# Pool's additions, their stores and a table load placed behind the next group's combinations

## The chip, the cores and the metric

The kernel runs on one core of one Trainium2 chip. The metric is device time in microseconds (us): the median of several executions. TensorE (PE in the profile, its weight loads PEld) multiplies matrices; VectorE (DVE), ScalarE (ACT) and GpSimd (POOL, called Pool here) work beside it, and SyncE (SP) issues most DMAs.

## The reference

The computation has two parts. First linear attention over batch 8, 8 heads, 576 tokens and head size 64; then an FNet block over the heads laid side by side (width 512):

```python
q_s = softmax(q, axis=-1); k_s = softmax(k, axis=2)        # each with + 1e-9 in the denominator
kv = einsum('bhsd,bhse->bhde', k_s, v)
x = einsum('bhsd,bhde->bhse', q_s, kv)                     # -> (B, S, H*D) = (8, 576, 512)

mixed = real(fft(fft(x, axis=1), axis=2))
u = x + mixed
un = (u - mean(u)) / sqrt(var(u) + 1e-6)                   # over the 512 columns
ch = relu(un @ w_ch1) @ w_ch2                              # 512 -> 2048 -> 512
return u + ch
```

## The kernel before, in words

The tokens are worked in nine groups of 512. Groups 0 to 7 hold 512 of the 576 tokens of one batch element each; group 8 (`B`) holds the 64 left over of all eight. They run in the order 0 to 6, 8, 7. While group g runs its two large products on TensorE, the attention, the Fourier mixing and the normalisation of later groups are worked in between.

Matrix products use a Strassen-Winograd scheme with seven products instead of eight; `ORDER = (1, 6, 5, 7, 2, 4, 3)` is the order of the seven. For the first product of a group (`up`, L1366, un @ w_ch1 and relu) the transposed, normalised u of the group lies in the tile `unT` in seven blocks: blocks 0 to 3 are quarters of u, and blocks 4, 5, 6 and a new block 1 are differences of them, 4 = 1 - 0, 1 = 3 - 1, 5 = 3 - 4, 6 = 2 - 5. `B_AT` says which block a product reads: m=1 block 0, m=6 block 5, m=5 block 4, m=7 block 1, m=2 block 2, m=4 block 6, m=3 block 3. `up` makes four passes (j = 0 to 3) over these seven products. Three PSUM banks carry them: ba (m=1, then m=2), bb (m=6, then m=7, then m=4, on top of each other) and bc (m=5, then m=3). Between two products of one bank DVE reads the bank (u2 and u3 at L1336, other results at L1377), so the next product of that bank waits for this reading.

The second product (`deep_down`, the matmuls of L1463 and L1493) is a Strassen scheme of two levels for the groups after group 1. The outer products come as 1, then the pairs (2, 4), (7, 6), (5, 3). The results of an inner scheme are put together by DVE (L1500) and ACT (L1507, L1514) into blocks of the tile `big`. From there they are added into `x`, which holds u, by `into` (L1443, 128x512 elements each); `sums` (L1446) adds two such blocks. Both run on `E`, which is Pool, except for the last two groups, where it is DVE. The list `after` gives each such step a time after its pair. Then `store` sends the finished rows out: rows in order go straight to `out_dram`, reversed ones through a DRAM tile `mirror`. Group 8's rows are put on a list, `later`, which `timed` empties during the last group, 36 DMAs, one every 1.2 units.

`norm(g)` prepares `unT` for a group while the group before is still in `deep_down`. DVE transposes 32x32 blocks (L1213) into spare blocks of `unT`; 32 small copies (`moved`, L1221), shared between ACT and Pool, put them in place; then `combine` (L1227) and `combine_last` (L1232) make the differences. `back` (L1181) has ACT load the table of the exponential again after the square root. At the same time the key part of a later attention runs (`keys`): maxima on DVE (L696), two exchanges of the maxima between partitions (ACT L676 and L679, each followed by a minimum on DVE, L683), exponentials on ACT (L700), transposes on DVE (L709), and matmuls (L716). The q part begins with a maximum (L757 on DVE) and a subtraction on Pool (L762).

The order of all this is written out by hand. Every step is a pair of a time in units and a function; a group takes 106 units. All steps are sorted by time and issued in that order, so each engine runs its own instructions in the order of these times, and waits, by semaphores, for what others have not finished. Times are not enforced; only the order counts. At a group's end the order of the steps of Pool, DVE and ACT, in units from the end of `deep_down` (which is the start of the next group's `up`), is:

```text
Pool  sums 7+6 at -9, into(1,0,7) at -7 among the copies of u (-11 to -5.3), into(1,1,7) at -5,
      block 1 at -3.9, into(1,1,5) at +1, into(0,1,5) at +2, into(0,1,3) at +4
DVE   blocks 4 and 5 at -3.9, L683 at -2.8, L1500 (bank bb) at -2.5, L683 at -1.6, L1500 (bc) at -0.5
ACT   table load at -11.9, copies of u until -5.3;   SP  stores at +3.5, +4.5, +7, +8
```

Of the kernel before, what the change touches and what calls it, by code (L numbers as in the profile page):

```python
# [43 lines left out]
ALU = mybir.AluOpType  # L44
# [75 lines left out]
def at(t, script):  # L120
    return [(t + dt, step) for dt, step in script]


def tokens(c, u):

    a = {(0, 0): 1, (0, 1): S - P, (1, 0): S // 2 - P, (1, 1): S // 2 + 1}[c, u]
    return slice(a, a + P)
# [11 lines left out]
class _Block:  # L139
# [1017 lines left out]
    def norm(self, g):  # L1157

        nc, V = self.nc, self.nc.vector
# [63 lines left out]
        def combine():  # L1223
            if g > 0:
                some = lambda i: self.unT[g][:, i]
                for e, to, x, y in ((V, 4, 1, 0), (nc.gpsimd, 1, 3, 1), (V, 5, 3, 4)):
                    e.tensor_tensor(out=some(to), in0=some(x), in1=some(y), op=ALU.subtract)  # L1227

        def combine_last():
            if g > 0:  # L1230
                some = lambda i: self.unT[g][:, i]
                V.tensor_tensor(out=some(6), in0=some(2), in1=some(5), op=ALU.subtract)  # L1232

        steps = []
        put = lambda t, f, *a: steps.append((t, lambda: f(*a)))
        if g > 1:
            for c in range(2):
                t = 7.5 * c
                for n, i in enumerate((c, c + 2)):
                    put(t + n, stats, i)  # L1240
                    put(t + 4.2 + n, normal, i)
                    put(t + 5.5 + n, turned, i)
                put(t + 2, root, slice(c, 4, 2))
                put(t + 3.2, scales, slice(c, 4, 2))
                for n in range(16):
                    put(t + 7.2 + .4 * n, moved, c, n % 4, n // 4)
            put(7.5 + 6.6, back)
            put(7.5 + 8.2 + 16 * .4, combine)
            put(7.5 + 18.2 + 16 * .4, combine_last)
            return steps  # L1250
        if g == 0:
# [13 lines left out]
        for n, i in enumerate((0, 2, 1, 3)):  # L1265
            put(9.3 + 1.3 * n, normal, i)
            put(11.8 + 1.3 * n, turn, i)
            put(12.6 + 1.3 * n, laid, i)
        put(17.5, combine)
        put(27.5, combine_last)  # L1270
        return steps
# [141 lines left out]
    def deep_down(self, g, order):  # L1413

        nc, V, G = self.nc, self.nc.vector, self.nc.gpsimd
        base, last, skip = self.base[order] + NP, order == B, self.first_deep(order)
# [8 lines left out]
        box, steps = {}, []  # L1425
# [22 lines left out]
        def store(t, u):  # L1448
            for c in range(2):
                steps.extend(at(t + c, self.store(g, c, u, lambda c=c: self.xpart(g, c, u))))  # L1450
# [25 lines left out]
        def half(t, c, u, d, wait=9):  # L1476
            x = lambda: self.xs[g, u][:, c, d * HD:(d + 1) * HD]
            steps.extend(at(t, self.store(g, c, u, x, d, wait)))
# [23 lines left out]
        def ends(unit, n):  # L1502
# [14 lines left out]
            if n == 3:  # L1517
                plus(out(1), "bc", "u2")

        after = {(2, 4): [(7, into, 1, 0, 4), (9, into, 0, 0, 2)],  # L1520
                 (7, 6): [(1, sums, 6, 1), (3, into, 0, 1, 6), (5, sums, 7, 6), (7, into, 1, 0, 7), (9, into, 1, 1, 7)],
                 (5, 3): [(0.6, into, 1, 1, 5), (1.2, into, 0, 1, 5), (1.8, into, 0, 1, 3)] if last else
                         [(1, into, 1, 1, 5), (2, into, 0, 1, 5), (4, into, 0, 1, 3)]}
        names = {1: ("bb", "bb"), 2: ("bc", "bb"), 4: ("ba", "bb")}
        n, t = 2 * len(ORDER), 0
        for i, unit in enumerate(order):
# [28 lines left out]
        if last:  # L1555
            half(t - 8 + 2, 1, 1, 1)
            half(t - 8 + 3, 0, 0, 1)
            half(t - 8 + 3.1, 1, 0, 1, 3)
        else:
            store(t + 3.5, 1)  # L1560
            store(t + 7, 0)
        return steps

    def down(self, g, order):
# [66 lines left out]
    def store(self, g, c, u, x, d=None, wait=9):  # L1631


        nc, own = self.nc, g < B
        e = nc.sync if d is None or c else nc.scalar
        s = slice(0, D) if d is None else slice(d * HD, (d + 1) * HD)
        if not own:
            def later():
                self.later += [lambda r=r, m=m: e.dma_start(m, x()[r]) for r, m in self.shared(self.out, 2 * (2 * u + c))]
            return [(0, later)]  # L1640
        out = self.out[g, tokens(c, u), s]
        if c == u:
            return [(0, lambda: self.apart(e.dma_start(out, x())))]
        box = []
        cols = lambda a: a.rearrange("t (k n) -> k t n", n=DH)

        def there():
            t = self.dram.tile([P, D], F32, tag="mirror", name="mirror", bufs=4)
            box.append(t[:, s])
            e.dma_start(box[0], x())  # L1650

        return [(0, there), (wait, lambda: self.apart(e.dma_start(cols(out)[:, ::-1, :], cols(box[0]))))]
# [3 lines left out]
def kernel(ctx: ExitStack, tc: tile.TileContext, q, kT, v, w1, w2, ft,  # L1656
                                                           cd, out):
    blk = _Block(ctx, tc, q, kT, v, w1, w2, ft, cd, out)

    def timed(t, order, g):  # L1660
        b = order + 1
        steps = at(t, blk.up(order, g)) + at(t + UP, blk.down(g, order))
        if order == B:
            return steps + [(t + 6 + 1.2 * i, lambda i=i: blk.later and blk.later.pop(0)()) for i in range(36)]
        if b == B:
            return steps + at(t + UP + 16, blk.norm(groups[b]))
        start, end = -7 if order > 2 else 0, 45
        if b + 1 < B:
            steps += at(t, blk.ahead(b + 1))
        steps += at(t, blk.attention_timed(b, start, end)) + at(t + end, blk.folded(b))  # L1670
        t, soon = t + UP, 2 * (order == 1)
        for i, k in enumerate((2, 3, 0, 1, 4)):
            steps += at(t + soon + (1.7 if order > 1 else 2) * i, blk.block(b, k))
        mixes = [blk.mix_own(b, c) for c in range(2)]
        if b % 2:
            mixes.insert(0 if b == B - 1 else 2, blk.mix_shared(b // 2))
        for i, some in enumerate(mixes):
            steps += at(t + 9.2 + 1.65 * soon + 3.2 * i, some)
        return steps + at(t + 24 + 1.65 * soon, blk.norm(groups[b]))
# [31 lines left out]
    steps = blk.opening(fetch, converted)  # L1711
# [3 lines left out]
    t = first + second  # L1715
# [28 lines left out]
    t = 0  # L1744
    for order, g in enumerate(groups[1:], 1):
        later += timed(t, order, g)
        t += UP + (TWICE if order > 1 else UP)
# [59 lines left out]
```

## Time and profile before

| | us |
|---|---|
| median of 3 runs (lowest, highest) | 1047.89 (1046.48, 1051.24) |
| the profiled execution's own time | 1048.45 |
| its span on the core | 1046.7 |
| PE busy | 1027.1 |
| DVE busy | 744.1 |
| ACT busy | 495.3 |
| POOL busy | 445.7 |
| granted TensorE clock, share of full | 0.998 |

The span is the time from the first to the last instruction of the program in the profiled execution. Busy times are of one engine each, and they overlap. In the list of waits a line names who waited, for whom, the total, how often, and the longest. In the timeline a line has the start, the length, the engine, the line of the kernel, what is written and read, the shapes, the count of instructions merged into the line, and in brackets the idle time before it with what ended it. In the table of windows the columns are the window, its length, then the busy time (and instructions) of PE, PEld, DVE, ACT and POOL, the granted clock, the DMA engines' mean busy share and the GB/s moved.

### The profile page before, as it was taken

What the parts mean: (1) busy time and instruction counts of PE and PEld (TensorE: products, weight loads), DVE (VectorE), ACT (ScalarE), POOL (GpSimd) and SP (SyncE); (2) the same over time, 40 slices, a digit from 0 to 9 for tenths busy, and PEclk for the clock granted to TensorE, in tenths of its full rate; (3) what the DMA queues carried; (4) which work ended last, traced back from release to release, by engine and by line L of the source; (5) the groups of instructions that cost most, each with busy time, mean ns of one, the idle gap of its engine ahead of it and who ended that gap; (6) DMA issues with size and microseconds to landing.
All of it is one profiled execution on the core that took longest, in us unless ns stands there. A gap on an engine that the chain in (4) does not pass through costs nothing.

```text
span 1046.7 us, 16845 instructions
## 1 busy us (share of the span) xinstructions
PE 1027.1 (98%) x6066; PEld 888.5 (85%) x6066; DVE 744.1 (71%) x1452; ACT 495.3 (47%) x1246; POOL 445.7 (43%) x448
## 2 busy tenths in 40 slices
PE   8999999999999999999999999999999999999998
PEld 7844554888888898889988998989898998999898
DVE  5898888775766897677776787579757754694463
ACT  5674532862449227842675256823682242151210
POOL 3164420366543736554736555474656470040000
PEclk9999999999999999999999999999999999999999
DMA  8787598587999566955786577747644674575464
GB/s 259 254 264 259 173 257 291 181 243 232 330 303 231 201 247 228 244 197 192 258 217 196 200 253 244 198 178 262 218 167 161 224 259 161 213 278 204 171 228 144
DMA packets 114315, 236.02 MB, mean 225 GB/s; under 512 B 23272, under 2 KB 78696, under 8 KB 103608
## 3 DMA queue, kind: packets, MB, share of 16 engines
q1 hardware_dynamic: 113864, 234.42, 68.4%
q8 instruction: 48, 0.79, 0.3%
q14 instruction: 35, 0.29, 0.1%
q10 hardware_dynamic: 288, 0.26, 0.1%
q0 software_dynamic: 80, 0.26, 0.1%
HBM read 199.79 MB, written 39.06 MB: 228 GB/s over the span
## 4 chain that ended last, share of the span: by engine, by line
PE 72%; DVE 9%; DMA 3%; ACT 3%; POOL 2%; issue 1%; SPq 0%; DVEq 0%; ACTq 0%; POOLq 0%
PE bb L1366 15%; PE ba L1366 9%; PE bc L1366 9%; PE bb L1493 8%; PE ba L1493 5%; PE bb L1463 5%; PE bc L1493 5%; PE bb L1582 2%; PE acc L791 2%; PE acc L716 2%; PE acc L1088 2%; PE acc L1091 1%; PE bc L1582 1%; PE ba L1582 1%; DMA big<-w1s 1%
## 5 line engine op out<-in xcount | busy, mean ns | idle before, releaser
L1366 PE MATMUL bb<-unT,big 128*128 128x256 f32 x768 | 182.7, 380 | 5.8 <-DVE big L1500 3.3
L1366 PEld LDWEIGHTS bb<-unT,big 128*128 128x128 f32 x768 | 143.8, 190 | 27.3 <-DVE big L1500 4.9
L1378 ACT ACTIVATE big<-big 128x512 f32<-128x512 f32 x96 | 60.3, 629 | 157.0 <-DVE big L1377 156.0
L775 ACT ACTIVATE qT<-q 32x128 f32<-32x128 f32 x384 | 117.9, 307 | 13.8 <-DVE q L765 8.7
L1366 PE MATMUL ba<-unT,big 128*128 128x256 f32 x512 | 124.0, 379 | 0.0
L1366 PE MATMUL bc<-unT,big 128*128 128x256 f32 x512 | 121.9, 380 | 0.0
L1366 PEld LDWEIGHTS bc<-unT,big 128*128 128x128 f32 x512 | 96.0, 190 | 13.5 <-DVE big L1377 1.1
L1366 PEld LDWEIGHTS ba<-unT,big 128*128 128x128 f32 x512 | 94.5, 190 | 12.0 <-issue 0.5
L1493 PE MATMUL bb<-big 128*128 128x128 f32 x848 | 104.2, 276 | 0.4 <-DVE u L1500 0.3
L1336 DVE TENSOR_TENSOR u<-bb,s 128x512 f32<-128x512 f32 x66 | 45.4, 689 | 81.6 <-PE bb L1366 68.6
L1493 PEld LDWEIGHTS bb<-big 128*128 128x128 f32 x848 | 98.9, 192 | 1.5 <-DVE u L1500 1.0
L1443 POOL TENSOR_TENSOR x<-x,big 128x512 f32<-128x512 f32 x45 | 59.9, 1340 | 55.9 <-ACT big L1470 18.8
L1221 POOL COPY unT<-unT 32x256 f32<-32x256 f32 x98 | 43.1, 440 | 91.1 <-DVE unT L1213 86.8
L1493 PE MATMUL ba<-big 128*128 128x128 f32 x640 | 78.0, 275 | 0.0
L1493 PEld LDWEIGHTS ba<-big 128*128 128x128 f32 x640 | 75.2, 192 | 0.7
L1439 DVE TENSOR_TENSOR big<-big 128x512 f32<-128x512 f32 x98 | 73.4, 780 | 0.0
L762 POOL TENSOR_TENSOR q<-q,qm 128x512 f32<-128x512 f32 x24 | 25.8, 1074 | 102.3 <-DVE qm L757 50.0
L1221 ACT COPY unT<-unT 32x256 f32<-32x256 f32 x126 | 50.6, 402 | 28.2 <-DVE unT L1213 26.5
L385 POOL TENSOR_TENSOR big<-big 128x512 f32<-128x512 f32 x24 | 30.5, 1270 | 69.4 <-ACT big L1378 69.4
L1463 PE MATMUL bb<-big 128*128 128x256 f32 x256 | 59.5, 380 | 0.0
L1377 DVE TENSOR_TENSOR big<-bc,u 128x512 f32<-128x512 f32 x64 | 44.0, 688 | 19.4 <-PE bc L1366 18.6
L1463 PEld LDWEIGHTS bb<-big 128*128 128x128 f32 x256 | 48.2, 190 | 8.3 <-DVE big L1377 1.1
(282 smaller groups left out, 2040.3 us busy)
## 6 DMA issues: line engine op xcount, KB each, us to landing
big<-w2d SPq DMA_DIRECT2D x67, 1024.0 KB
big<-w1s SPq DMA_DIRECT2D x64, 896.0 KB
big<-w2s SPq DMA_DIRECT2D x16, 1024.0 KB
big<-in_w_dram SPq DMA_DIRECT2D x21, 512.0 KB
w2d<-big SPq DMA_DIRECT2D x42, 256.0 KB
kb<-in_kT_dram SPq DMA_DIRECT2D x24, 320.0 KB
q<-in_q_dram SPq DMA_DIRECT2D x28, 256.0 KB
vt<-in_v_dram SPq DMA_DIRECT2D x36, 160.0 KB
```

The lines of the kernel that those rows point to most:

```text
L385: e1.tensor_tensor(out=to(4), in0=at(2), in1=at(3), op=ALU.add)
L775: nc.scalar.activation(to[t, i * Q:i * Q + Q], one, ACT.Exp)
L1221: copy(to, of)
L1336: plus = lambda t: V.tensor_tensor(out=temp(t), in0=box["bb"][:], in1=box["s1"][:], op=ALU.add)
L1366: nc.tensor.matmul(bank()[:, i, :], lhsT=w[:, WA_AT[m], k * P:(k + 1) * P], rhs=self.unT[g][:, B_AT[m], k, :], start=first and i == 0 and ...
L1377: steps = [(0, lambda: V.tensor_tensor(out=hp(i), in0=bank()[:], in1=u()[:], op=ALU.add)), (0.8, lambda: nc.scalar.activation(hp(i), hp(i) ...
L1378: (0.8, lambda: nc.scalar.activation(hp(i), hp(i), ACT.Relu))]
L1439: e.tensor_tensor(out=to(o), in0=to(x), in1=to(y), op=op)
L1443: E.tensor_tensor(out=x, in0=x, in1=tile(m), op=ALU.add)
L1463: nc.tensor.matmul(box[name][:, i, :], lhsT=h[p][:, A_AT[m], i * P:(i + 1) * P], rhs=self.stream[n][:, p, :], start=p == 0 and (m != 1 or ...
L1493: nc.tensor.matmul(box[place[n]][:, i, :], lhsT=own(m)(A_AT[n])[:, f, :], rhs=w[:, r // 2, r % 2 * P:r % 2 * P + P], start=first and f == ...
L1582: nc.tensor.matmul(bank()[:, i, :], lhsT=h[p][:, A_AT[m], i * P:(i + 1) * P], rhs=w[:, p, :], start=first and i == 0 and p == 0, stop=p == ...
```

## The change

For groups with g > 1 Pool makes block 5 (3 - 4), which was DVE's, and DVE makes block 1 (3 - 1), which was Pool's. Block 1 gets a step of its own, `combine_one`, at +0.6 units. ACT's table load moves behind the copies of u (from -11.9 to -4.7). In all groups but the last the two additions of result 7 leave the place among the copies, and all five additions of the group's end stand at +4, +5.5, +7, +8.5 and +10. The stores move from +3.5 and +7 to +9.5 and +13 (with their second halves one unit later). The list of group 8's stores is emptied from 11 units on instead of 6.

```diff
         def combine():
             if g > 0:
                 some = lambda i: self.unT[g][:, i]
-                for e, to, x, y in ((V, 4, 1, 0), (nc.gpsimd, 1, 3, 1), (V, 5, 3, 4)):
+                for e, to, x, y in ((V, 4, 1, 0), (nc.gpsimd, 5, 3, 4)) if g > 1 else ((V, 4, 1, 0), (nc.gpsimd, 1, 3, 1), (V, 5, 3, 4)):
                     e.tensor_tensor(out=some(to), in0=some(x), in1=some(y), op=ALU.subtract)
+
+        def combine_one():
+            some = lambda i: self.unT[g][:, i]
+            V.tensor_tensor(out=some(1), in0=some(3), in1=some(1), op=ALU.subtract)
...
-            put(7.5 + 6.6, back)
+            put(7.5 + 7.4 + 16 * .4, back)
             put(7.5 + 8.2 + 16 * .4, combine)
+            put(7.5 + 12.7 + 16 * .4, combine_one)
             put(7.5 + 18.2 + 16 * .4, combine_last)
...
-                 (7, 6): [(1, sums, 6, 1), (3, into, 0, 1, 6), (5, sums, 7, 6), (7, into, 1, 0, 7), (9, into, 1, 1, 7)],
+                 (7, 6): [(1, sums, 6, 1), (3, into, 0, 1, 6), (5, sums, 7, 6), *(((7, into, 1, 0, 7), (9, into, 1, 1, 7)) if last else ())],
                  (5, 3): [(0.6, into, 1, 1, 5), (1.2, into, 0, 1, 5), (1.8, into, 0, 1, 3)] if last else
-                         [(1, into, 1, 1, 5), (2, into, 0, 1, 5), (4, into, 0, 1, 3)]}
+                         [(4, into, 1, 0, 7), (5.5, into, 1, 1, 7), (7, into, 1, 1, 5), (8.5, into, 0, 1, 5), (10, into, 0, 1, 3)]}
...
-            store(t + 3.5, 1)
-            store(t + 7, 0)
+            store(t + 9.5, 1)
+            store(t + 13, 0)
...
-            return steps + [(t + 6 + 1.2 * i, lambda i=i: blk.later and blk.later.pop(0)()) for i in range(36)]
+            return steps + [(t + 11 + 1.2 * i, lambda i=i: blk.later and blk.later.pop(0)()) for i in range(36)]
```

## The prediction

> **What bounds the kernel now.** I read the page's engine shares first, then TensorE's waits, then windows over the group ends, then the timeline of one group end engine by engine.
>
> ```profile
> PE 1027.1 (98%) x6066; PEld 888.5 (85%) x6066; DVE 744.1 (71%) x1452; ACT 495.3 (47%) x1246; POOL 445.7 (43%) x448
> ...
> PE bb L1366 <- DVE big L1500: 3.3, 4, 0.9
> PE bb L1366 <- DVE u L1336: 2.5, 4, 0.6
> ```
>
> TensorE is busy for 98% of the span, so only its idle time can be won, and of that 5.8 us are two waits that occur four times each. Both belong to the first products of a new group. The windows give their full price. Each runs from a group's first matmul to the start of its fifth product (m=2):
>
> ```profile
> 404.73:415.90 11.17, 9.65 (x55) 8.31 (x53) 8.46 (x16) 8.30 (x29) 6.15 (x5) 1.00 0.69 256
> 517.05:528.07 11.02, 9.64 (x55) 8.30 (x53) 8.31 (x16) 6.49 (x21) 7.41 (x6) 1.00 0.63 241
> 629.54:640.70 11.16, 9.64 (x54) 8.30 (x53) 8.45 (x16) 8.30 (x29) 6.12 (x5) 1.00 0.72 256
> 741.83:752.86 11.03, 9.65 (x54) 8.31 (x53) 8.32 (x16) 6.50 (x21) 7.43 (x6) 1.00 0.62 238
> 854.64:861.55 6.91, 6.91 (x34) 6.03 (x33) 3.52 (x5) 0.59 (x1) 6.41 (x5) 1.00 0.80 302
> ```
>
> The last row has the same four products without attention work and without a wait: 6.91 us, 1.73 a product. The other four rows also hold two runs of ten attention matmuls (L716), 1.12 us each by the timeline below (526.95 to 528.07). Without waits they would take 6.91 + 2 x 1.12 = 9.15. So they lose 2.02, 1.87, 2.01 and 1.88, together 7.8 us, at a granted clock of 1.00. This is more than the 5.8 of the wait list, because the pipe also restarts after each wait.
>
> The timeline of the second of these ends (first matmul at 517.05), in the order PE, DVE, POOL, ACT:
>
> ```profile
> 517.05 1.89 PE L1366 MATMUL ba<-unT,big 128*128 128x256 f32 x8
> 519.69 1.99 PE L1366 MATMUL bb<-unT,big 128*128 128x256 f32 x8 [0.75 <-DVE big L1500]
> 525.15 1.96 PE L1366 MATMUL bb<-unT,big 128*128 128x256 f32 x8 [0.63 <-DVE u L1336]
> 526.95 1.28 PE L716 MATMUL acc<-vt,kb 128*128 128x129 f32 x10
> ...
> 512.69 2.26 DVE L696 TENSOR_REDUCE km<-kb 128x4 f32<-128x640 f32 x3
> 515.78 2.37 DVE L1227 TENSOR_TENSOR unT<-unT 128x512 f32<-128x512 f32 x2 [0.83 <-POOL unT L1221]
> 518.07 1.23 DVE L683 TENSOR_TENSOR km<-km,across 128x16 f32<-128x16 f32 x1
> 519.22 0.41 DVE L1500 TENSOR_TENSOR big<-bb,s 128x256 f32<-128x256 f32 x1
> 523.59 0.84 DVE L709 STREAM_TRANSPOSE kb<-kb 128x640 f32<-128x640 f32 x1 [0.91 <-ACT kb L700]
> 524.36 0.65 DVE L1336 TENSOR_TENSOR u<-bb,s 128x512 f32<-128x512 f32 x1
> ...
> 513.58 1.27 POOL L1443 TENSOR_TENSOR x<-x,big 128x512 f32<-128x512 f32 x1
> 515.83 1.77 POOL L1443 TENSOR_TENSOR x<-x,big 128x512 f32<-128x512 f32 x1
> 517.56 1.71 POOL L1227 TENSOR_TENSOR unT<-unT 128x512 f32<-128x512 f32 x1
> ...
> 519.33 0.84 ACT L679 COPY across<-km 32x16 f32<-32x16 f32 x4 [3.93 <-DVE km L683]
> 520.41 1.70 ACT L700 ACTIVATE kb<-kb,km 128x160 f32<-128x160 f32 x5 [0.24 <-DVE km L683]
> ```
>
> Stall one: product m=6 needs PSUM bank bb, which DVE's L1500 empties only at 519.63. That addition's input was ready near 515.5 (L1493 moves on to bank bc at 515.26), but it stands in DVE's queue behind the two combinations (2.37 us, of which the second takes 1.64 where 0.69 is normal) and a 16-column minimum (L683, 1.23 where its median is 0.18). Both slow ones lie beside Pool's L1443 and L1227 and end just after them: a DVE operation with two SBUF inputs and a Pool operation do not overlap here, one waits for the other. Stall two: m=7 overwrites bb and needs u2 (L1336), which stands behind the key transposes (L709), which need ACT's exponentials (L700), which start at 520.41 because that same minimum was late.
>
> **The change, part by part,** on this group end (times as above).
>
> Pool before the combination. One addition into x (513.58, 1.27) leaves from among the copies of u. The last two copies (0.83) then follow at 513.58 and end at 514.41, not 515.74.
>
> ACT. The table load (1.28) and its dummy activation (0.20) leave from before nine copies, which end at 514.29, and go behind them. The copies end near 512.8, the load fills 512.8 to 514.3, and the next copy (L1514, 514.31) starts as now. Cost nothing; its cover is that L1514 waits for PE's ba anyway.
>
> First combination on DVE (block 4). It is no longer gated by Pool but by DVE's own key maxima, which end at 514.95: 514.95 to 515.65, 0.8 earlier. Block 5, which stood next on DVE, goes to Pool. So L683 follows at 515.7 (its inputs are there: ACT's L676 copies, issued at 514.98, take 0.42) and L1500 at 515.9 to 516.3. Bank bb is free 2.5 us before m=6 wants it at 517.05 + 1.73 = 518.78. Stall one goes.
>
> Block 5 on Pool. It waits for block 4 (515.65). A Pool subtraction of this shape has no undisturbed row; the bounds are 1.27 (L1443 alone) and 1.77 (L1443 beside a DVE combination). Nothing but the short L683 stands beside it, so I take 1.27 to 1.45: done by 517.2, at most 517.5. m=6 reads it at 518.78: hidden, with 1.3 us or more to spare. Behind it in Pool's queue are only the additions into x.
>
> The second stall's chain. ACT's L679 copies run 516.0 to 516.85; the second minimum waits until Pool lets go, about 517.2; L700 starts near 517.5 instead of 520.41. Five exponentials (1.70 with 0.33 a step), the s1 copy (0.56) and three more end near 520.7; the transpose (0.84) ends at 521.5, u2 (0.65) at 522.2. m=7 wants bank bb at 517.05 + 3 x 1.73 + 1.12 = 523.35. Stall two goes with 1.1 us to spare. What is late next is u3, by the same shift at 526.2 to 527, against m=4 at 517.05 + 5 x 1.73 + 2 x 1.12 = 527.9.
>
> Block 1 on DVE (new third combination) stands between L1500's second addition and the first transpose. It takes 0.69, or up to 1.64 if it meets an addition of Pool's: done by 519.1. The first transpose needs four exponentials (518.8), so at most 0.3 us is added there, and m=7 reads block 1 at 523.35. Hidden.
>
> Pool's five additions (1.27 each, 1.77 beside DVE) come at 517.2 and later instead of 513.58 to 524.74. Two run at once, three come behind the next q subtraction (L762, which waits for a DVE maximum), and the last ends near 529. The regions of big they read are next written by the new group's m=3 result (start of its addition 12 us after 517.05) or by Pool itself later in order. Nobody waits.
>
> Stores. SP puts four stores out of x, and two out of mirror, later, behind the four vt loads, which wait for PE (528.26 now, 526.4 then). Four stores at 0.35 to 0.45 us of issue each are out before the weight load that waits for the end of the first pass. The buffers of x are next written by DVE's L804 at 27.8 us after the first matmul; the last mirror copy now leaves at about 14.5 and needs a few us. The stores (4 x 256 KB, about 3 us of transfer) move from a stretch in which the DMA engines are little used (share 0.34 in 526 to 529) toward the full one (1.18 in 543 to 550, 0.97 in 550 to 556). Then they idle (0.29 in 556 to 562.5), before the weights asked for at 548.69 are needed at about 562.5. Room of some 4 us against 3, with weights ahead of vt in the queue: taken as nothing, and kept for a rival.
>
> Other ends. At 293.45, 854.64 and 948.48 TensorE has no wait at the first products; there the move is worth 0, with about 1 us of cover for Pool's block (at 293.45 the present Pool combination ends at 294.36, m=6 starts at 295.18). At 941.23 a wait of 0.26 may go. At 948.48 the five additions are DVE's, and fall into idle gaps of about 2 us. The 36 stores of group 8 start five units later and still end before the last group's w2d loads.
>
> Sum: 7.8 us, against the profiled execution: span 1046.7 to 1038.9, with 1.75 around it 1048.45 to 1040.65. That execution is 0.56 above the median of the three runs, so 1047.89 - 7.8 = 1040.1.
>
> One rule bears against the change. The Trainium skill's page "SBUF — State Buffer", section "SBUF: two separate sides", says that the pair of ports shared by VectorE and GpSimd is an exclusive lock: whichever starts first holds it for the whole instruction, and the other is blocked entirely. The stretched rows above (0.69 to 1.64, 0.18 to 1.23) agree. By it Pool's work packed behind 515.7 would block L683 twice; what that gives is the first rival.
>
> **Rivals.** *Second stall stays.* If Pool's block 5 starts before DVE's first L683, that waits to 517.0, the L679 copies end at 517.9 and the second L683 waits for an addition to 518.4. L700 starts at 518.6, and u2 ends at 523.4 with m=7 wanting 523.35; one more blocked operation (1.27) brings stall two back whole. The gain is then stall one: (519.69 - 518.78) plus about 0.1 of restart, near 1.02 and 1.15 in turn, 4.3 in all: 1043.6. For it: the two L683 slowed to 1.23 in every end. Against: where both wait for the end of the same combination (172.04), DVE's next starts at 172.08 and Pool's at 172.18.
>
> *A wait on Pool replaces stall one.* m=6 waits for block 5 as long as it waits now for the bank; with stall two partly there, 1047 to 1048. It needs Pool 1.3 us later than worked out; nothing in Pool's queue supplies that.
>
> *Slower: weights late.* The moved stores reach the full DMA stretch and push the weights of the fourth pass past 562.5. It decides once they come more than about 4 us later than now; at 3 us moved plus 1.9 of earlier demand it is not out of reach. Each us beyond costs one in each of four groups; 4 us beyond, with the gain of 7.8 given back, is 1047.9 + 16 - 7.8 = 1056. Against: SP's issues of weights wait for PE, not for DMA, and the weights stand ahead of the vt loads, which nobody needs then.
>
> **How the numbers follow.** Both stalls gone 0.72 (own range 1038.5 to 1042.3: from 0.7 more by small waits, to 0.3 to 0.5 left of stall two in each end); only the first 0.14, at 1043.6; replaced 0.06, near 1047.5; slower 0.08, near 1056. About 0.5% (5.2 us, the spread of the runs before) can be told from no change, so faster 0.75 (the first and a little of the second), same 0.17, slower 0.08. The range 1038.2 to 1045 takes in the first two cases and leaves out 0.14.
>
> **What the profile after would show.** Right: no wait of PE on L1500 or on L1336's u at the four ends; windows of about 9.15 us to the fifth product; DVE's L1227 at about 0.69 each, the first 2.1 us before the group's first matmul; L700 about 0.5 after it (3.4 now). Wrong: a PE wait on Pool's L1227, a PE wait on DMA big<-w1s in the fourth pass, or DVE waiting on DMA before L804.

## The result, and the profile after

The changed kernel takes 1038.57 us (median of 6 runs, 1037.82 to 1040.01) against 1047.1 of the kernel before on the same chip (6 runs, 1046.42 to 1051.24): a ratio of 0.9916, 95% interval 0.9898 to 0.9933, or 8.5 us less. 7.8 less had been forecast, from 1047.89. The profiled execution took 1039.82, with a span of 1038.0.

The page's first line on the engines and two lines of the list of TensorE's waits, of the changed kernel:

```profile
PE 1023.7 (99%) x6066; PEld 888.8 (86%) x6066; DVE 736.4 (71%) x1452; ACT 496.1 (48%) x1246; POOL 441.7 (43%) x448
...
PE ba L1371 <- DMA big<-w1s: 1.3, 1, 1.3
...
PE bb L1498 <- DVE u L1505: 0.2, 1, 0.2
```

(The change adds lines: L1371 here is L1366 before, L1505 is L1500, L1341 is L1336, L1448 is L1443, L1498 is L1493, L1383 is L1378; L1231 is the new combination of block 1.) Both waits on bank bb, four times each, are gone. There is one wait that the profile before does not have, for weights. The windows from a group's first matmul to its fifth product (first its length, then the engines' busy time, the granted clock, the DMA share and GB/s):

```profile
405.40:414.53 9.13, 9.13 (x54) 8.30 (x53) 7.60 (x14) 7.73 (x25) 5.27 (x4) 1.00 0.53 202
515.27:524.42 9.15, 9.15 (x55) 8.32 (x54) 7.62 (x14) 5.72 (x17) 5.53 (x5) 1.00 0.47 175
625.89:635.02 9.13, 9.13 (x54) 8.30 (x53) 7.60 (x14) 7.73 (x25) 5.26 (x4) 1.00 0.54 206
735.74:744.90 9.16, 9.16 (x55) 8.33 (x54) 7.63 (x14) 5.73 (x17) 5.54 (x5) 1.00 0.46 170
```

PE is busy for the whole of each window, and each is 9.13 to 9.16 long where 9.15 was forecast. The DMA share in them fell to 0.46 to 0.54 (0.62 to 0.72 before): the four stores out of `x`, which left SP 5.1 to 8.1 us after the first matmul of the second end before, now leave at 10.7 to 14.0, behind the window. The timeline of the second of these ends, whose first matmul is at 515.27 now (517.05 before), PE, DVE, POOL and ACT in turn:

```profile
517.00 1.89 PE L1371 MATMUL bb<-unT,big 128*128 128x256 f32 x8
521.57 1.89 PE L1371 MATMUL bb<-unT,big 128*128 128x256 f32 x8
...
513.09 0.68 DVE L1227 TENSOR_TENSOR unT<-unT 128x512 f32<-128x512 f32 x1
513.69 0.17 DVE L683 TENSOR_TENSOR km<-km,across 128x16 f32<-128x16 f32 x1
513.78 0.42 DVE L1505 TENSOR_TENSOR big<-bb,s 128x256 f32<-128x256 f32 x1
519.60 0.65 DVE L1341 TENSOR_TENSOR u<-bb,s 128x512 f32<-128x512 f32 x1
...
513.85 1.26 POOL L1227 TENSOR_TENSOR unT<-unT 128x512 f32<-128x512 f32 x1 [1.28 <-DVE km L683]
515.08 2.95 POOL L1448 TENSOR_TENSOR x<-x,big 128x512 f32<-128x512 f32 x2
...
515.18 1.70 ACT L700 ACTIVATE kb<-kb,km 128x160 f32<-128x160 f32 x5 [0.45 <-DVE km L683]
```

DVE's first combination, the minimum and the emptying of bank bb now follow each other, and bb is free 2.8 us before m=6 (517.00). Pool starts block 5 only after the minimum, 0.16 later than the minimum starts, and ends it 1.9 us before m=6. ACT's exponentials start 0.09 us before the group's first matmul; they started 3.36 after it. u2 ends at 520.25, 1.3 us before m=7.

For the whole run I put the 6066 matmuls of both profiles side by side, as they come in the same order, and took how far each starts from its counterpart. From the first matmul of group 3 to the last of all the changed kernel gains 9.15 us: 2.44, 1.88, 2.44 and 1.91 in groups 3 to 6, 0.49 in group 8 and nothing in group 7. Ahead of group 3 it is 0.67 behind: 0.35 gained in the opening, where nothing was changed, and 1.02 lost in group 2, by the wait for weights.

### The profile page after: what moved, and what is told of

The parts are those of the page before. It is cut to its first block, busy times and chain, and to the rows that moved or that the text cites. A ratio compares the mean times of both kernels' runs of the same rounds, so it can differ in the third digit from the quotient of the medians.

```text
span 1038.0 us, 16852 instructions
## 1 busy us (share of the span) xinstructions
PE 1023.7 (99%) x6066; PEld 888.8 (86%) x6066; DVE 736.4 (71%) x1452; ACT 496.1 (48%) x1246; POOL 441.7 (43%) x448
## 4 chain that ended last, share of the span: by engine, by line
PE 89%; DVE 5%; DMA 3%; ACT 1%; issue 0%; SPq 0%; POOL 0%; POOLq 0%; DVEq 0%; ACTq 0%
PE bb L1371 15%; PE ba L1371 10%; PE bc L1371 10%; PE bb L1498 10%; PE ba L1498 7%; PE bc L1498 7%; PE bb L1468 5%; PE acc L716 2%; PE bb L1587 2%; PE bc L1308 2%; PE acc L1088 2%; PE acc L791 2%; PE bb L1287 2%; DMA big<-w1s 2%; PE ba L1287 2%; PE bc L1287 2%
## 5 line engine op out<-in xcount | busy, mean ns | idle before, releaser
L1371 PE MATMUL bb<-unT,big 128*128 128x256 f32 x768 | 181.9, 379 | 0.0
L1371 PEld LDWEIGHTS bb<-unT,big 128*128 128x128 f32 x768 | 144.3, 190 | 19.3 <-DVE u L1341 0.5
L1383 ACT ACTIVATE big<-big 128x512 f32<-128x512 f32 x96 | 60.3, 629 | 157.4 <-DVE big L1382 156.4
L1371 PE MATMUL ba<-unT,big 128*128 128x256 f32 x512 | 124.1, 379 | 1.3 <-DMA big<-w1s 1.3
L1371 PE MATMUL bc<-unT,big 128*128 128x256 f32 x512 | 121.7, 379 | 0.0
L1371 PEld LDWEIGHTS bc<-unT,big 128*128 128x128 f32 x512 | 96.1, 190 | 13.2 <-DVE big L1382 0.5
L1371 PEld LDWEIGHTS ba<-unT,big 128*128 128x128 f32 x512 | 94.5, 190 | 13.5 <-DMA big<-w1s 1.5
L1341 DVE TENSOR_TENSOR u<-bb,s 128x512 f32<-128x512 f32 x66 | 45.4, 688 | 84.0 <-PE bb L1371 71.0
L1498 PE MATMUL bb<-big 128*128 128x128 f32 x848 | 104.1, 276 | 0.2 <-DVE u L1505 0.2
L1498 PEld LDWEIGHTS bb<-big 128*128 128x128 f32 x848 | 98.9, 192 | 1.1 <-DVE u L1505 0.6
L1448 POOL TENSOR_TENSOR x<-x,big 128x512 f32<-128x512 f32 x45 | 59.3, 1333 | 49.2 <-ACT big L1475 19.4
L1498 PE MATMUL ba<-big 128*128 128x128 f32 x640 | 78.0, 275 | 0.0
L1498 PEld LDWEIGHTS ba<-big 128*128 128x128 f32 x640 | 75.2, 192 | 0.7
```

Of the source, the lines that this page charges most:

```text
L1341: plus = lambda t: V.tensor_tensor(out=temp(t), in0=box["bb"][:], in1=box["s1"][:], op=ALU.add)
L1371: nc.tensor.matmul(bank()[:, i, :], lhsT=w[:, WA_AT[m], k * P:(k + 1) * P], rhs=self.unT[g][:, B_AT[m], k, :], start=first and i == 0 and ...
L1383: (0.8, lambda: nc.scalar.activation(hp(i), hp(i), ACT.Relu))]
L1448: E.tensor_tensor(out=x, in0=x, in1=tile(m), op=ALU.add)
L1498: nc.tensor.matmul(box[place[n]][:, i, :], lhsT=own(m)(A_AT[n])[:, f, :], rhs=w[:, r // 2, r % 2 * P:r % 2 * P + P], start=first and f == ...
```

## Experiments

Four theories were set against each other. **Port**: DVE's two-input operations and Pool's hold each other up, and the stalls come from what that does to the order of DVE's queue. **Gate**: the gain is the earlier start of the first combination. **Relief**: DVE had one combination too many ahead of the bank. **Chance** is about the wait for weights alone: it comes and goes with the way the transfers fall. Besides each median I give the gain from group 3's first matmul on, by the matmuls side by side, which leaves the opening and group 2 out.

### The table load alone

```diff
-            put(7.5 + 6.6, back)
+            put(7.5 + 7.4 + 16 * .4, back)
```

> The kernel before with ACT's table load alone moved behind the copies of u. Port theory (the stalls come from DVE operations held by Pool's two-input operations): no change, 1047 to 1048, since the first combination is gated by Pool's last copy (515.74 in the profile before), not by ACT's (514.29); ACT's copies end 1.5 us earlier and nothing follows from it. Gate theory (the gain comes from an earlier first combination, and ACT's copies are part of its gate): up to 0.8 us in each of six group ends, 1043.

Measured: 1048.51 (1047.36 to 1050.42) against 1047.57, ratio 1.0009, interval 0.9999 to 1.0018; from group 3 on 0.15 gained. (In the profile 0.43 are lost in group 2, by the same wait for weights.) DVE's combinations and Pool's last copies at the second group end, whose first matmul is at 516.48:

```profile
515.19 2.36 DVE L1227 TENSOR_TENSOR unT<-unT 128x512 f32<-128x512 f32 x2 [0.80 <-POOL unT L1221]
...
514.33 0.83 POOL L1221 COPY unT<-unT 32x256 f32<-32x256 f32 x2
```

ACT's copies end early and nothing follows, since the first combination still waits for Pool's copies, and the pair still takes 2.36. The load is free in both places, as forecast.

### The exchange of blocks 1 and 5 alone

```diff
-for e, to, x, y in ((V, 4, 1, 0), (nc.gpsimd, 1, 3, 1), (V, 5, 3, 4)):
+for e, to, x, y in ((V, 4, 1, 0), (nc.gpsimd, 5, 3, 4)) if g > 1 else (...):
...
+            put(7.5 + 12.7 + 16 * .4, combine_one)
```

(against the kernel before; the function `combine_one` is the one of the change)

> The kernel before with the exchange of blocks 1 and 5 alone: Pool's additions, the stores and the table load stay. Port theory: Pool's block 5 stands behind one addition into x and ends near 519.0 to 519.3 in the group end at 517.05, so m=6 waits 0.3 to 0.6 us for it instead of 1.0 for the bank; L700 starts about 0.9 us earlier, and stall two shrinks to about 0.4. Gain about 1 us in each of four ends, 1043. Gate theory: no gain, 1047, since the first combination starts when it did. Relief theory (DVE had one combination too many ahead of the bank's reading, and that is all): the whole gain, 1039.

Measured: 1041.81 (1041.29 to 1042.18) against 1047.57, ratio 0.9947, interval 0.993 to 0.9963; from group 3 on 6.18. DVE, then POOL, at the same group end, whose first matmul is at 514.38; and one of TensorE's waits:

```profile
513.07 0.69 DVE L1227 TENSOR_TENSOR unT<-unT 128x512 f32<-128x512 f32 x1 [0.79 <-POOL unT L1221]
513.68 1.24 DVE L683 TENSOR_TENSOR km<-km,across 128x16 f32<-128x16 f32 x1
514.84 0.41 DVE L1505 TENSOR_TENSOR big<-bb,s 128x256 f32<-128x256 f32 x1
...
513.12 1.77 POOL L1448 TENSOR_TENSOR x<-x,big 128x512 f32<-128x512 f32 x1
514.85 1.27 POOL L1227 TENSOR_TENSOR unT<-unT 128x512 f32<-128x512 f32 x1
...
PE bb L1371 <- POOL unT L1227: 0.5, 1, 0.5
```

The addition still stretches the minimum to 1.24. But there is no second combination behind it to be stretched as well, so bb is free at 515.25 and block 5 there at 516.12, just when m=6 wants it (514.38 + 1.73): stall one leaves 0.05 to 0.2 in each end, and stall two is gone but for 0.09. My 0.3 to 0.6 and 0.4 were too much: I had block 5 end 1.9 to 2.2 us after the first matmul, with some of the stretch of Pool's row before (1.71). It takes 1.27, with only L1505 of DVE's beside it, which reads a PSUM bank, and ends 1.74 after. In the end at group 8, which had no stall before, m=6 now waits 0.5 for Pool: the rival in which a wait on Pool takes the place of stall one is real where the additions stay in front. Gate falls by this run, since the first combination starts 1.3 us before the first matmul, as it did before, and two thirds of the gain are there. Relief, which wanted the whole gain, falls short by the other third: 0.26 to 0.39 stay in each of the four ends, the transposes of q (L913) still wait 0.28 in groups 3 and 5, and 0.26 is lost in group 8, where the changed kernel gains 0.49.

### The additions, stores and the list alone

```diff
-for e, to, x, y in ((V, 4, 1, 0), (nc.gpsimd, 5, 3, 4)) if g > 1 else (...):
+for e, to, x, y in ((V, 4, 1, 0), (nc.gpsimd, 1, 3, 1), (V, 5, 3, 4)):
-            put(7.5 + 7.4 + 16 * .4, back)
+            put(7.5 + 6.6, back)
-            put(7.5 + 12.7 + 16 * .4, combine_one)
```

(against the changed kernel)

> The changed kernel with blocks 1 and 5 made where they were before (5 on DVE, 1 on Pool) and the table load where it was: the additions, stores and the list of group 8's stores alone are moved. Port theory: the first combination starts 0.8 us earlier and the second takes 0.69; then Pool's block 1 holds the first L683 for about 1.3 us and an addition holds the second for about 0.4, so stall one goes, and of stall two 0.5 to 0.9 us stays: 1042 to 1043.5. Gate theory: the whole gain, 1039.

Measured: 1041.48 (1040.49 to 1042.28) against 1047.57, ratio 0.9945, interval 0.9928 to 0.9962; from group 3 on 6.04. DVE and POOL at the second group end, first matmul at 513.38, and one of TensorE's waits:

```profile
511.20 1.41 DVE L1227 TENSOR_TENSOR unT<-unT 128x512 f32<-128x512 f32 x2
512.53 1.24 DVE L683 TENSOR_TENSOR km<-km,across 128x16 f32<-128x16 f32 x1
...
511.97 1.77 POOL L1227 TENSOR_TENSOR unT<-unT 128x512 f32<-128x512 f32 x1 [1.27 <-DVE unT L1227]
...
PE tr L913 <- DVE q L885: 1.6, 2, 0.8
```

The second combination takes its 0.69 again, and block 1 on Pool holds the minimum instead. Both stalls go, the second by a hair where I had expected 0.5 to 0.9 of it. The loss shows elsewhere: DVE's chain runs about 1.2 us later than in the changed kernel, and in groups 3 and 5 the transposes of q (L913) wait 0.8 for it, where they wait 0.2 in the kernel before and 0 in the changed one. So the total came near (1041.48, and 1042 to 1043.5 was expected), and its place was wrong. Each half of the change gives 6.0 to 6.2 and both together 9.15: either half makes room enough on DVE for most of both stalls, and the other half takes the rest.

### The changed kernel without the moved table load

```diff
-            put(7.5 + 7.4 + 16 * .4, back)
+            put(7.5 + 6.6, back)
```

(against the changed kernel)

> The changed kernel with the table load back where it was, among the copies of u. Port theory: as the changed kernel, 1038.6, within 0.1%: ACT's copies then end 0.66 us before DVE's key maxima, which gate the first combination. Gate theory: 0.3 to 0.8 us of loss in each end, 1040 to 1043.

Measured: 1041.1 (1040.01 to 1042.34) against 1047.57, ratio 0.9935, interval 0.9919 to 0.9952. By the median the gate theory would have won. The matmuls side by side say otherwise: from group 3 on 9.15, to the hundredth as in the changed kernel. In the profiled execution (1042.34) the loss lies in group 2: 3.89 there, where the fourth pass waits for its weights, and 1.02 in the changed kernel's own profile. A window just after that wait and TensorE's timeline there:

```profile
341.80:346.00 4.20, 4.16 (x12) 3.38 (x13) 0.00 (x0) 0.59 (x1) 4.12 (x5) 0.62 0.99 362
...
341.84 1.19 PE L1371 MATMUL ba<-unT,big 128*128 128x256 f32 x4 [2.07 <-DMA big<-w1s]
342.82 3.56 PE L1371 MATMUL bb<-unT,big 128*128 128x256 f32 x8
```

The wait is 2.07, and after it the granted clock is 0.62: eight matmuls take 3.56 us instead of 1.89. At the group ends the load's old place costs nothing. The landing times listed under the next experiment don't show that it makes the wait more likely either: in the five profiles with the load at its old place (before, exchange alone, additions alone, without the load, one addition moved) they run from -3.2 to +0.7, in the six with the load behind the copies from -3.2 to +0.4.

### The changed kernel again, and with the key loads later

The second kernel changes one number, so that the four loads of keys in group 2 are issued behind the weights of the fourth pass and not among them:

```diff
-        steps = at(20 if b == 2 else 27 if b < 5 else 24, self.keys_to(b))
+        steps = at(20 if b == 2 else 27 if b < 4 else 33 if b == 4 else 24, self.keys_to(b))
```

(against the changed kernel)

> The changed kernel itself, on the chip of the next three. The profiles so far show one wait that comes and goes: the fourth pass of group 2 (near 340 us) waits 0 to 2.1 us for its weights, also where nothing before that place was changed. Theory of chance (DMA transfers of that stretch have no room and end now earlier, now later): 1038 to 1040, and some wait there in some profiles. Theory of the table load (the changed kernel is faster than the one without the moved load by 2.5 us): 1038.5 here too, with less spread than that.

> The changed kernel with the four loads of keys in group 2 put behind the weights of its fourth pass instead of among them (six units later). Theory of chance: the weights land some us earlier, the wait near 340 us is 0 in the profile, and the median falls by 0.3 to 1.5 us against the changed kernel, with a smaller spread. Theory that the transfers ahead of the weights are not what delays them: no difference, and the wait appears as often.

> The changed kernel with group 2's four key loads behind the fourth pass's weights, once more beside the changed kernel. In its first profile the last packet of those weights landed 9.9 us ahead of the pass; in nine profiles with the old place it was between 3.2 us late and 0.7 early. Theory of chance: again 9 to 10 us early, no wait near 340 us, and a median 0.3 to 1.5 us below the changed kernel of the same call. Rival (the median of the first time, 1.0 lower, was the chip's own scatter): the same as the changed kernel, though the weights land early.

> The changed kernel, for the comparison with the run ahead of it: 1038.5 to 1039.5; the fourth pass's weights of group 2 land between 3 us late and 1 us early.

Measured the first time: 1039.44 (1036.87 to 1040.56) unchanged and 1038.43 (1036.97 to 1039.66) with the keys later; the second time 1040.13 (1038.04 to 1040.72) and 1038.41 (1037.15 to 1039.79). From group 3 on all four gain 9.11 to 9.18. How early the last packet of weights (7168 bytes) ended before the fourth pass of group 2 began, worked out from the traces' DMA packets, in us; below zero the packet came after the pass had begun:

```text
keys at their old place   before +0.7   changed -2.3, -0.3, -1.0   table load alone -1.3
                          exchange alone -0.8   additions alone +0.4   without the load -3.2
                          the three kernels below, in turn, -3.2, -2.1, +0.4
keys later                +9.9, +8.6
```

Kernels whose instructions are the same up to there stand apart: the exchange alone and the one without the load at -0.8 and -3.2; the kernel before, the additions alone and the one addition moved at +0.7, +0.4 and -2.1. So the wait comes and goes from one execution to the next, and the late keys remove it: the DMA engines' share in the stretch ahead (316 to 340) is 0.95 in the profile before and 0.98 in the changed one, and the keys stood in front of the weights. In the times it is worth about 0.9 us (means of nine and ten runs, 1038.48 and 1039.41). The runs of one kernel scatter by more than that, so the gain in time is likely, not shown; the earlier landing is shown. No version had a lower median, but the changed kernel itself (1038.57 above) and the one with the stores later still (1038.56) lie as low within the scatter.

### All three combinations on DVE

```diff
-((V, 4, 1, 0), (nc.gpsimd, 5, 3, 4)) if g > 1
+((V, 4, 1, 0), (V, 5, 3, 4)) if g > 1
```

(against the changed kernel)

> The changed kernel with block 5 back on DVE, behind block 4, and nothing of the combinations on Pool. Port theory: nothing now holds Pool's additions back, so the first starts with the last copy done and holds block 4 for about 0.8 us, the second holds block 5 for about 1.2; stall one stays away by a little, L700 starts about 2 us later than in the changed kernel, stall two comes back at 0.5 to 0.7, and the q transposes of every second end wait 0.8: 1041.5 to 1043. Theory that only the earlier start of the combinations counts: as the changed kernel, 1038.6.

Measured: 1043.94 (1042.71 to 1046.11) against 1047.84, ratio 0.9959, interval 0.9945 to 0.9973; from group 3 on 4.70. The median lies above the 1041.5 to 1043 expected; in the profile 3.35 are lost in group 2, by the wait for weights. DVE and POOL at the second end (first matmul at 518.75), and one of TensorE's waits:

```profile
516.57 3.05 DVE L1227 TENSOR_TENSOR unT<-unT 128x512 f32<-128x512 f32 x2
...
516.12 2.95 POOL L1448 TENSOR_TENSOR x<-x,big 128x512 f32<-128x512 f32 x2
...
PE bb L1371 <- DVE u L1341: 1.3, 4, 0.4
```

With nothing of its own to wait for, Pool begins its additions at once, and two combinations that take 1.41 undisturbed take 3.05. Stall one stays away, stall two comes back at 0.25 to 0.39, and L913 waits 0.85 in groups 3 and 5. What the exchange does, then, is not only to take work off DVE. Pool's block 5 waits for DVE's block 4, and while Pool waits, its additions wait behind it.

### One addition moved

```diff
-(5, sums, 7, 6), (7, into, 1, 0, 7), (9, into, 1, 1, 7)],
+(5, sums, 7, 6), (7, into, 1, 0, 7), *(((9, into, 1, 1, 7),) if last else ())],
-[(1, into, 1, 1, 5), (2, into, 0, 1, 5), (4, into, 0, 1, 3)]}
+[(0.9, into, 1, 1, 7), (1, into, 1, 1, 5), (2, into, 0, 1, 5), (4, into, 0, 1, 3)]}
```

(against the kernel before)

> The kernel before with one of Pool's additions, the one that lies beside the two combinations, put behind Pool's block 1; all else as before. Port theory: DVE's second combination takes 0.69 instead of 1.64 and its first L683 is held by block 1 instead; bank bb is emptied 0.9 us earlier, stall one falls from 1.0 to 0.1 or 0.2, and stall two stays (0.6 to 0.9): 1043 to 1044.5. Theory that a subtraction in unT is slow of itself: no change, 1047.5.

Measured: 1044.99 (1044.45 to 1048.0) against 1047.84, ratio 0.9976, interval 0.9964 to 0.9988; from group 3 on 3.12. The median lies 0.5 above the 1043 to 1044.5 expected, and 0.86 are lost in group 2 in the profile. DVE at the second end, and one of TensorE's waits:

```profile
514.89 1.42 DVE L1227 TENSOR_TENSOR unT<-unT 128x512 f32<-128x512 f32 x2 [0.85 <-POOL unT L1221]
516.23 1.24 DVE L683 TENSOR_TENSOR km<-km,across 128x16 f32<-128x16 f32 x1
...
PE bb L1366 <- DVE u L1336: 3.2, 4, 0.8
```

Moving one 1.27 us addition of Pool's past Pool's own combination shortens DVE's pair from 2.37 to 1.42, and stall one is gone (0.91 to 0.99 gained in each of four ends); stall two stays, at 0.8 instead of 0.63, since block 1 still holds the minimum (1.24). That is the port theory in its smallest form: no DVE instruction was touched.

### The stores later still

```diff
-            store(t + 9.5, 1)
-            store(t + 13, 0)
+            store(t + 19.5, 1)
+            store(t + 23, 0)
-    return steps + [(t + 11 + 1.2 * i, ...
+    return steps + [(t + 21 + 1.2 * i, ...
```

(against the changed kernel)

> The changed kernel with the stores at each group's end, and the emptying of group 8's list, ten units later still. Theory of room (a store hurts nobody until something waits for its buffer or its transfer): x's buffer is written again by DVE's L804 about 26 us after the first matmul, and the last copy out of x now leaves SP at about that time, so L804 waits for it, DVE's later readings of the banks stand behind L804, and TensorE waits 1 to 3 us in each of five groups: 1043 to 1052. The weights of the fourth pass keep about the room that they have. Rival (stores are free wherever they stand): 1038 to 1040.

Measured: 1038.56 (1037.9 to 1045.07) against 1048.32, ratio 0.9923, interval 0.9892 to 0.9953; from group 3 on 9.13. My expectation missed. The last copy out of x leaves SP 20.0 to 24.9 us after the first matmul, and L804 writes the buffer at 26.0 to 28.0 and does not wait. The stores have at least the 10 units more of room that this run gives them.

## Why the prediction was right

**The two stalls** were sized right and went as worked out. Forecast per group 2.02, 1.87, 2.01 and 1.88; measured 2.44, 1.88, 2.44 and 1.91, of which 0.38 in each 2.44 is the wait of the q transposes (L913, 0.22 in the profile before, and its restart), which I had not put into the sum. Group 8 adds 0.49, from the wait of 0.26 near 941 and its restart, which I had said may go. Together these are most of the 1.35 between 7.8 and 9.15. What the last matmul shows is 8.49, because of the wait for weights and the opening. So the mechanism was right, and that the total came within 0.7 is in part luck: 1.35 more was won than counted, and ahead of group 3 1.02 was lost in a wait that the sum didn't have, of which the opening gave back 0.35. (The spread of the runs before, put at 5.2 us in the prediction, is 4.8: 1046.48 to 1051.24.)

**The chain of steps**, as distances from the group's first matmul. First combination: forecast -2.1, measured -2.18. Bank bb empty: -0.75, measured -1.08. Block 5 ready: 0.15 to 0.45, measured -0.15, by an undisturbed 1.26. L700: 0.45, measured -0.09. u2: 5.15, measured 4.98. Block 1 done: 2.05, measured 1.63. Pool's last addition: near 12, measured 11.6. Taking the nearest undisturbed row for Pool's subtraction was right here, where of DVE's only a reading of a PSUM bank and the end of a minimum stood beside it.

**The lock.** The rival built on the Trainium skill's page "SBUF — State Buffer" needed Pool to start before DVE's first L683. It did not, by a margin of 0.16 in each of the four ends (513.85 against 513.69 here), and L683 took 0.17. The traces agree with the rule: with a Pool instruction running, DVE's minimum took 1.24 in three experiments (exchange, additions, one addition) and ended 0.03 us after that instruction, and the pair of combinations took 3.05 in a fourth. The prediction cited the rule only against the change; it is also why the change works.

**Weights late.** The mechanism is there, and the room was larger than the 4 us or so that I had taken: the moved stores bring the fourth pass's weights from 5.0, 7.6 and 7.2 us ahead of need in groups 3 to 5 to 2.8, 3.4 and 3.9 in the profile after, and to 2.7, 4.7 and 4.5 in that of the changed kernel again. They are not late there. The wait that did appear, a PE wait on big<-w1s in a fourth pass, is one that the prediction had named as a sign of being wrong. It is in group 2, which the moved stores don't touch, and where the kernel before had 0.7 us to spare; I had not looked at that group's margin.

**Free parts.** The table load, the new combination on DVE and the other group ends cost nothing, as forecast, and the stores nothing but room.

## What to carry to other kernels

When an engine that is never the bound runs two-input work on SBUF beside another engine's short, urgent operations, look at the durations of those: an operation that takes 0.17 alone and 1.24 in place is not slow but held, and what to move is the neighbour. An instruction that must wait for the urgent engine, put at the head of the neighbour's queue, keeps the neighbour out of the way; here it cost nothing. And set two profiles side by side matmul by matmul: the medians said that the table load was worth 2.5 us, the traces showed the same gain to the hundredth from group 3 on and the difference in one wait for a transfer ahead of it.

## What the runs showed of the hardware that was not expected

**A short wait can halve TensorE's clock.** After waits of 2.07 and 1.97 us for weights the granted clock was 0.62 and 0.59 in the 4 us that followed, and matmuls took nearly twice their time (eight in 3.56 us instead of 1.89); after 1.31 and 1.02 it stayed at 1.00. So the 2.07 us cost 3.9. The Trainium skill's page "TensorE: Matmul & The Clock Gate", section "Part 1: The HAM clock gate (the "warmup" mystery)", puts the limit at an idle window of about 3.4 us. Here the gap in the profile was shorter than that. Nor does the length of the gap alone decide it. In the opening, where TensorE has other short gaps, a wait of 1.21 (at 15.83, keys later again) was followed by a clock of 0.50 from 17.09 to 20.50, and one of 1.27 (at 11.66, changed kernel a third time) by 1.00. The stretches at 0.50 after the waits of 2.07 and 1.97 were just as long (342.78 to 346.19 and 342.07 to 345.49).

**A small DVE operation with one SBUF input is held too.** L875 (TENSOR_SCALAR, 128x8) takes 0.17 in group 3 of the profile before, at 420.18, and 0.74 in the same place of the changed kernel, at 417.73, where one of Pool's additions (417.18 to 418.44) stands beside it. The q chain on DVE has 0.3 us to spare for it there: L885 ends 14.03 us after the group's first matmul, and L913 starts at 14.32.
